# A delta-rule attention with two MLP layers on one core: full-width weight conversion in place, own token staging, masks fused into evacuations, copies that may go to GpSimd

## The chip, the cores and the metric

The kernel runs on one core of one Trainium2 chip. The metric is the device time of one execution in microseconds. TensorE (PE) multiplies, VectorE (DVE), ScalarE (ACT) and GpSimd (POOL) do the elementwise work, SyncE (SP) issues all DMAs.

## What is computed

A delta-rule recurrence over 768 positions for 4 batches of 8 heads with head size 48, and then two MLP layers over all 3072 tokens with a width of 384 and 2048 hidden units. The inputs are float64; the weights come as pairs of 32-bit words and are converted on the core.

```python
for t in range(S):                         # S = 768, state is 48 x 48 per head
    kt, vt, bt = (k_n[:, :, t], v[:, :, t], beta[:, :, t, None])
    y[:, :, t] = np.einsum('bhd,bhde->bhe', q[:, :, t], state)
    v_old = np.einsum('bhde,bhd->bhe', state, kt)
    state = state + bt[:, :, :, None] * np.einsum('bhd,bhe->bhde', kt, vt - v_old)
# x: tokens x 384
h = x @ w_in;  g = np.where(h >= 1, h, np.where(h <= -1, 0, (h + 1) ** 2 / 4));  x = g @ w_out
h = x @ w2_in; g = h * np.clip(h + 3, 0, 6) / 6;                                 x = g @ w2_out
```

`k_n` is k divided by its norm.

## The kernel before

The sequence is cut into 12 chunks of 64 positions. For each chunk `front(c)` loads k twice (once by position into KN, once as tokens into ST), loads q into ST and v into E, takes the norms, transposes the tokens on TensorE, and forms the products of k with k and with q (`products`, two halves of the heads, hb = 0 and 1). `inverse(c)` inverts a triangular matrix for every head: on 32-wide blocks by a row of small multiply and subtract steps (L566, L571; on VectorE for chunk 0, on GpSimd for the rest), and the rest by matmuls. `chain(c)` is the serial part: it computes E from the inverse (L705), the next state, and y, which goes to XB as two parts, a high and a low one. Part of y passes through YS and six small DMAs (L786) into XB.

MLP layer 1 runs in blocks of one chunk (the first two) or two chunks, layer 2 in six blocks of 512 tokens. For each of the 16 slices f of 128 hidden units there are H matmuls (`mlp_h`), a nonlinearity on ScalarE and VectorE (GF, GH, GL), and O matmuls (`mlp_o`). All MLP matmuls are made three times, with weights and activations each split into a high and a low part.

The weights of a slice f are prepared by `wload`: five DMAs (three in layer 2) into a raw buffer (RAWL with four slots, RAWR with one), and then six operations on each half of 384 columns: scale the high words (into TBS), mask the sign bits out of them (L826, into a second buffer), round the low words into 16 bits of that buffer (L828, ScalarE), shift and combine (L831, VectorE), copy the high part into WLA or WLB, subtract to get the low part. Layer 1 is prepared while the first chunks run.

ST has two buffers, so a half's k and q tokens wait until the half before has been transposed. The masked products (p of q with k) are evacuated by ScalarE without a mask (L514) or by VectorE with the mask (L516); for those of ScalarE, a second pass multiplies by the mask in SBUF (L535, VectorE or GpSimd).

The order of everything is made ahead of time by `Plan.emit`. Each operation has a cost, a priority and a choice of engines; the planner puts the operation with the earliest start next, and each engine then runs its queue in that order. Until the first MLP matmul, TensorE's gaps are filled with matmuls on GH that compute nothing. `PR` holds the priorities, and a bias per engine. `cpalt` is a copy that may run on one of several engines, `ttalt` a two-input operation.

```python
AD = PR["ad"]                      # copies: ACT or DVE
DP = PR["dp"]; DW = PR["dw"]       # masks and scalings: DVE or POOL; weight subtraction: DVE
```

Of the kernel before, what the change touches and what calls it, by code (L numbers as in the profile page):

```python
# [37 lines left out]
class Plan:  # L38
# [1104 lines left out]
```

## Time and profile before

| | |
|---|---|
| median of 3 runs | 1086.45 us (1084.42 to 1089.5) |
| profiled execution | 1090.76 us, span 1089.0 us |
| TensorE busy | 1045.1 us (96%) |
| VectorE busy | 662.6 us (61%) |
| ScalarE busy | 595.7 us (55%) |
| GpSimd busy | 277.6 us (25%) |
| TensorE's mean granted clock | 0.983 of 2.4 GHz |

Busy shares over the whole span hide that the stages differ: the attention fronts and the weight conversion lie in the first 600 us and most of all in the first 200, and the end is MLP alone. Times in the rows below are counted from the start of the span. A row of a timeline may hold several equal instructions (x2). A mean in a group is that of one instruction; neighbours on one engine overlap a little, so a sum of means is larger than the busy time. What ended an engine's idle time stands behind the arrow.

### The profile page before, as it was taken

How to read it: one execution, taken by the hardware profiler on the slowest of the kernel's cores; microseconds unless marked ns; L12 is line 12 of the kernel's file. 1: busy time of each engine (PE TensorE's matmuls, PEld its weight loads, DVE VectorE, ACT ScalarE, POOL GpSimd, SP SyncE). 2: the span in 40 equal slices, each digit the busy share in tenths (PEclk: the TensorE clock that was granted, in tenths of full speed). 3: DMA queues.
4: the chain of work that ended last, by engine and by line, in shares of the span. 5: the costliest groups of instructions: out<-in, count | busy, mean ns of one | idle time of the engine just before them, and what ended most of it. 6: DMA issues, size and time to landing. Idle time of an engine off the chain costs nothing.

```text
span 1089.0 us, 25916 instructions
## 1 busy us (share of the span) xinstructions
PE 1045.1 (96%) x10684; PEld 890.1 (82%) x10684; DVE 662.6 (61%) x1258; ACT 595.7 (55%) x1164; POOL 277.6 (25%) x652
## 2 busy tenths in 40 slices
PE   8985899999999999999999999999999999999998
PEld 6764888887777778778778788898999998999897
DVE  4969778777869767786855589533333333333332
ACT  4768686766668576765755689433323232322322
POOL 3022313084755858548460000000000000000000
PEclk9987899999999999999999999999999999999999
DMA  9963243231314303322122284402011020200000
GB/s 179 191 142 66 61 99 66 45 63 36 59 21 97 69 17 59 90 45 46 40 57 83 80 257 139 116 1 88 1 41 47 1 87 2 59 29 1 29 1 29
DMA packets 174757, 71.86 MB, mean 66 GB/s; under 512 B 121264, under 2 KB 170544, under 8 KB 174640
## 3 DMA queue, kind: packets, MB, share of 16 engines
q1 hardware_dynamic: 174640, 70.22, 27.1%
q8 instruction: 84, 1.38, 0.6%
q14 instruction: 33, 0.27, 0.1%
HBM read 53.68 MB, written 14.16 MB: 62 GB/s over the span
## 4 chain that ended last, share of the span: by engine, by line
PE 72%; DVE 11%; ACT 5%; DMA 4%; POOL 3%; issue 3%; SPq 1%; DVEq 0%; POOLq 0%; ACTq 0%
PE bank L389 71%; DMA RAWL<-in_moe_w_in_dram 2%; DVE X L506 2%; POOL TL L571 1%; POOL TMP L566 1%; ACT KQ L514 1%; DVE GF L880 1%; PE bank L471 1%; DVE KQ L535 1%; DMA RAWR<-in_moe_w_in_dram 1%; DVE GL L357 1%; DVE DL L624 1%; ACT G L366 1%; SPq L815 1%; DVE XB L777 1%
## 5 line engine op out<-in xcount | busy, mean ns | idle before, releaser
L389 PE MATMUL bank<-XB,WLA 128*128 128x512 f32 (+1 forms) x1404 | 341.2, 386 | 13.4 <-DMA XB<-YS 7.1
L389 PEld LDWEIGHTS bank<-XB,WLA 128*128 128x128 f32 x1404 | 251.9, 193 | 62.1 <-ACT TBS L828 6.6
L357 DVE TENSOR_TENSOR GL<-GF,GH 128x512 fp32r<-128x512 f32 (+1 forms) x208 | 139.4, 671 | 82.9 <-PE bank L389 57.4
L884 DVE SCALAR_TENSOR_TENSOR GF<-GF,bank 128x512 f32<-128x512 f32 x96 | 66.1, 688 | 193.0 <-ACT GF L883 192.9
L366 ACT ACTIVATE GH<-GF 128x512 fp32r<-128x512 f32 (+1 forms) x202 | 120.9, 599 | 114.3 <-DVE GF L884 69.1
L883 ACT ACTIVATE GF<-bank 128x512 f32<-128x512 f32 x96 | 57.5, 599 | 204.5 <-PE bank L389 203.6
L566 POOL TENSOR_TENSOR TMP<-TL,DL 128x126 f32<-128x126 f32 (+25 forms) x293 | 113.0, 386 | 115.8 <-DVE DL L624 65.7
L571 POOL TENSOR_TENSOR TL<-TL,TMP 128x126 f32<-128x126 f32 (+25 forms) x293 | 126.6, 432 | 23.0
L389 PE MATMUL bank<-GH,WLA 128*128 128x512 f32 (+1 forms) x504 | 121.5, 373 | 2.6 <-DVE GH L368 1.5
L389 PE MATMUL bank<-XB,WLB 128*128 128x512 f32 (+1 forms) x468 | 112.4, 382 | 0.2 <-DVE GF L880 0.2
L389 PE MATMUL bank<-WLA,GH 128*128 128x384 f32 x576 | 112.3, 336 | 0.0
L389 PEld LDWEIGHTS bank<-WLA,GH 128*128 128x128 f32 x576 | 102.8, 188 | 6.4
L389 PEld LDWEIGHTS bank<-GH,WLA 128*128 128x128 f32 x504 | 85.9, 192 | 20.7 <-ACT GH L366 3.5
L389 PEld LDWEIGHTS bank<-XB,WLB 128*128 128x128 f32 x468 | 83.4, 191 | 15.5 <-DVE GF L880 0.4
L880 DVE SCALAR_TENSOR_TENSOR GF<-bank,GF 128x512 f32<-128x512 f32 (+1 forms) x112 | 68.6, 612 | 45.0 <-ACT GF L879 43.8
L878 ACT ACTIVATE GF<-bank 128x512 f32<-128x512 f32 (+1 forms) x112 | 59.8, 534 | 60.6 <-PE bank L389 56.1
L389 PE MATMUL bank<-GL,WLA 128*128 128x512 f32 (+1 forms) x252 | 65.9, 370 | 0.0
L879 ACT ACTIVATE GF<-GF 128x512 f32<-128x512 f32 (+1 forms) x112 | 63.5, 567 | 2.4
L389 PE MATMUL bank<-WLA,GL 128*128 128x384 f32 x288 | 61.5, 334 | 0.0
L389 PEld LDWEIGHTS bank<-WLA,GL 128*128 128x128 f32 x288 | 51.0, 188 | 0.0
L389 PE MATMUL bank<-GH 128*128 128x512 f32 x176 | 50.8, 437 | 0.0
L389 PEld LDWEIGHTS bank<-GL,WLA 128*128 128x128 f32 x252 | 43.9, 191 | 8.2 <-issue 0.3
(135 smaller groups left out, 1357.6 us busy)
## 6 DMA issues: line engine op xcount, KB each, us to landing
XB<-X SPq DMA_DIRECT2D x36, 256.0 KB, 4.7
X<-XB SPq DMA_DIRECT2D x30, 256.0 KB, 2.6
KN<-in_k_dram SPq DMA_DIRECT2D x24, 192.0 KB, 4.0
ST<-in_k_dram SPq DMA_DIRECT2D x48, 96.0 KB, 3.1
ST<-in_q_dram SPq DMA_DIRECT2D x48, 96.0 KB, 3.3
E<-in_v_dram SPq DMA_DIRECT2D x24, 192.0 KB, 3.8
RAWL<-in_moe_w_out_dram SPq DMA_DIRECT2D x12, 384.0 KB, 4.2
KQ<-in_moe_w_in_dram SPq DMA_DIRECT2D x12, 384.0 KB, 5.2
```

What stands on the lines that cost most here:

```text
L357: alts[e] = (d, lambda e=e: ENG[e].tensor_tensor(out=val(out), in0=val(in0), in1=val(in1), op=op))
L366: lambda: nc.scalar.activation(out=val(out), in_=val(in_), func=AF.Copy, scale=scale))
L389: nc.tensor.matmul(o, l, r, start=start, stop=stop)
L471: nc.tensor.transpose(bk.tile[0:112, p * 128:(p + 1) * 128], ST[i][:, p, 0:112], IDN)
L506: P.op("dve", 335, lambda bk=bk, u0=u0, rr=rr, ro=ro: nc.vector.tensor_tensor(out=X[rr, u0:u0 + NP, :], in0=bk.tile[ro].rearrange("p (a x) ...
L566: P.op(te, d, lambda t=t, s=s, r0=r0, a0=a0, a1=a1, m=m: ve.tensor_tensor(out=t[:, a0:a1], in0=TL[:, r0 + a0:r0 + a1, s:s + 1].to_broadcas ...
L571: P.op(te, d, lambda t=t, s=s, r0=r0, a0=a0, a1=a1: ve.tensor_tensor(out=TL[:, r0 + a0:r0 + a1, 0:s], in0=TL[:, r0 + a0:r0 + a1, 0:s], in1 ...
L878: P.op("act", da, lambda: nc.scalar.activation(out=gf, in_=ps, func=AF.Relu, scale=0.5, bias=0.5), r=[hkey(hb)], w=[gk], prio=MP)
L879: P.op("act", da + 48, lambda: nc.scalar.activation(out=gf, in_=gf, func=AF.Square), w=[gk], r=[gk], prio=MP)
L880: P.op("dve", 1.06 * n + 60, lambda: nc.vector.scalar_tensor_tensor(out=gf, in0=ps, scalar=1.0, in1=gf, op0=ALU.max, op1=ALU.min), r=[hkey ...
L883: P.op("act", da, lambda: nc.scalar.activation(out=gf, in_=ps, func=AF.Relu, scale=1.0 / 6.0, bias=0.5), r=[hkey(hb)], w=[gk], prio=MP)
L884: P.op("dve", 1.06 * n + 60, lambda: nc.vector.scalar_tensor_tensor(out=gf, in0=gf, scalar=1.0, in1=ps, op0=ALU.min, op1=ALU.mult), r=[hke ...
```

## The change

Five things change. (1) `wload` converts all 768 columns of a slice at once, so each step is one instruction and not two, and waits for all of the slice's DMAs. The sign bits are masked in place, and the rounded low words are written into the raw buffer too, so the second temporary is gone. The subtraction may also go to GpSimd (`dw`). (2) Chunks 0 and 1 get staging of their own: their second half's k and q tokens go to halves of G[0] and G[1], which are cleared for it, and the zeros that G needs are written later, by `zero_g`. (3) An evacuation of p on ScalarE is charged 500 ns more in the planner's choice (`me`), so more of them go to VectorE with the mask. (4) SBUF copies of X, LT and the diagonal blocks of G may go to GpSimd (`c3`). (5) The planner gets other costs for DMAs, holds back bulk loads while the DMAs are busy (`bulk`, `back`), and has other priorities.

```diff
-PR = dict(kv=-2.451, tok=-1.879, ... bias=27.418, biasa=601.736, hyst=4058, margin=800, dw=('dve',), ...)
+PR = dict(kv=-2.566, tok=-1.896, ... bias=33.201, biasa=369.235, hyst=4974.141, fgap=150, me=500, c3=('act', 'dve', 'pool'), back=1500, margin=251.294, dw=('dve', 'pool'), ...)
...
+                    if o["bulk"]:
+                        t = max(t, dma_free - PR["back"])
...
-                        end = t + o["alts"][e][0] + bias.get(e, 0.0)
+                        ex = o["extra"]
+                        end = t + o["alts"][e][0] + bias.get(e, 0.0) + ex.get(e, 0.0)
...
         for e in engs:
-            if e == "act":
+            if e == "pool":
+                alts[e] = (190 + 1.1 * n, lambda: nc.gpsimd.tensor_copy(val(out), val(in_)))
+            elif e == "act":
...
+    gs = [G[i].rearrange("p u e s -> p (u e s)") for i in range(2)]
+    extra = [gs[0][:, 0:512], gs[0][:, 512:1024], gs[1][:, 1024:1536], gs[1][:, 1536:2048]]
+    ST += [x.rearrange("p (a x) -> p a x", a=NP) for x in extra]
...
-        i = stage[0] % NST
+        if c < 2:
+            i = (0 if hb == 0 else 2 + 2 * c) + stage[0] % 2
+        else:
+            i = stage[0] % NST
...
-                                      q=qd(SH[dl], PO[g][dl], SH[dl]))
+                                      q=qd(SH[dl], PO[g][dl], SH[dl]), extra={"act": PR["me"]})
...
-            cpalt(AD, 256, X[p0:p0 + 32, us, 0:32], X[p0:p0 + 32, us, 32:64], False,
+            cpalt(PR["c3"], 256, X[p0:p0 + 32, us, 0:32], X[p0:p0 + 32, us, 32:64], False,
...
-                cpalt(AD, 512, LT[p0:p0 + 32], X[p0:p0 + 32, :, 32:64], False, ...)
+                cpalt(PR["c3"], 512, LT[p0:p0 + 32], X[p0:p0 + 32, :, 32:64], False, ...)
...
-        for pc in range(2):
...
-            tb, s_ = tmps[n % 2]
-            lw, hw = hl[:, 0, sl[0]:sl[1]], hl[:, 1, sl[0]:sl[1]]
+        tb = tmps[n % 2]
+        lw, hw = hl[:, 0], hl[:, 1]
+        low = raw.bitcast(I16).rearrange("p (n t) -> p t n", t=4)[:, 2]
+        need = [rkey] + [rkey + (i,) for i in range(len(parts))]
+        W = 2 * DM
+        cpalt(AD, W, tb.bitcast(F32), hw.bitcast(F32), False, 2.0 ** -112, r=need, w=[tk], prio=prio)
+        P.op("dve", 67 + 0.53 * W, lambda: V.tensor_scalar(
+            out=hw, in0=hw, scalar1=-2147483648, scalar2=None, op0=ALU.bitwise_and), r=need + [tk], w=[sk], prio=prio, port=("dve",))
+        P.op("act", 110 + 0.835 * W, lambda: nc.scalar.activation(
+            out=low, in_=lw.bitcast(U32), func=AF.Relu, scale=0.875 * 2.0 ** -29, bias=0.49),
+            r=need + [sk], w=[sk], prio=prio)
+        P.op("dve", 64 + 1.05 * W, lambda: V.scalar_tensor_tensor(
+            out=tb, in0=tb, scalar=3, in1=hw, op0=ALU.logical_shift_left, op1=ALU.bitwise_or), ...)
...
+    def zero_g(s_):
+        zk = [("zg", s_)] + [("gw", s_, hb, dl) ...] + tkeys(s_, 0) + tkeys(s_, 1) + [("st", 2 + 2 * s_ + i, b) for i in range(2) for b in range(2)]
+        zero(G[s_][32:64, :, 0, :], zk, 1200)
+        zero(G[s_][32:64, :, 1, 0:32], zk, 600)
+        zero(G[s_][96:128, :, 0, 0:32], zk, 600)
...
+        if c < 2:
+            zero_g(c)
         load_v(c)
```

How the change moves instructions shows at three places. The first is SyncE's queue after the first loads of chunk 0, before (the numbers behind names tell buffers apart: ST_78 and ST_79 are the two buffers of tokens, E_71 and KN_76 are those of even chunks, KN_77 of odd ones):

```order
L411 DMA ST_78<-in_k_dram 64x8x48 x2
L411 DMA ST_79<-in_q_dram 64x8x48 x2
L429 DMA E_71<-in_v_dram 64x16x48 x2
L422 DMA KN_77<-in_k_dram 64x16x48 x2
L815 DMA RAWL<-in_moe_w_in_dram 48x3x256
L815 DMA RAWL<-in_moe_w_in_dram 16x3x256
L815 DMA RAWL<-in_moe_w_in_dram 48x3x256
L815 DMA RAWL<-in_moe_w_in_dram 16x3x256
L411 DMA ST_78<-in_k_dram 64x8x48 x2
L411 DMA ST_79<-in_q_dram 64x8x48 x2
L815 DMA RAWL<-in_moe_w_out_dram 128x768
```

and with the change (here G_74 and G_75 stage tokens):

```order
L442 DMA E_71<-in_v_dram 64x16x48
L424 DMA G_74<-in_k_dram 64x8x48 x2
L424 DMA G_74<-in_q_dram 64x8x48 x2
L442 DMA E_71<-in_v_dram 64x16x48
L435 DMA KN_77<-in_k_dram 64x16x48 x2
L424 DMA ST_78<-in_k_dram 64x8x48 x2
L424 DMA ST_79<-in_q_dram 64x8x48 x2
L424 DMA G_75<-in_k_dram 64x8x48 x2
L424 DMA G_75<-in_q_dram 64x8x48 x2
```

The second half's tokens of chunk 0 stood behind E, KN_77 and the first weights; now they stand behind one half of E.

The second place is VectorE's queue where the small steps of chunk 0's inverse begin (L566 and L571 before, which are L579 and L584 after). Before:

```order
L587 STREAM_TRANSPOSE DL<-X 128x512
L357 TENSOR_TENSOR WLA<-TBS,WLA 128x384
L593 TENSOR_SCALAR DL<-DL,PAR 128x256
L831 SCALAR_TENSOR_TENSOR TBS<-TBS 128x384
L595 SCALAR_TENSOR_TENSOR DL<-DL,PAR 128x256
L368 CAST WLA<-TBS 128x384
L566 TENSOR_TENSOR TMP<-TL,DL 128x15
L357 TENSOR_TENSOR X<-KN_77 128x768
L571 TENSOR_TENSOR TL<-TL,TMP 128x15
L357 TENSOR_TENSOR WLA<-TBS,WLA 128x384
L566 TENSOR_TENSOR TMP<-TL,DL 128x28
L443 TENSOR_REDUCE SM<-X 128x16
```

and with the change:

```order
L606 TENSOR_SCALAR DL<-DL,PAR 128x256
L608 SCALAR_TENSOR_TENSOR DL<-DL,PAR 128x256
L362 TENSOR_TENSOR X<-KN_77 128x768
L579 TENSOR_TENSOR TMP<-TL,DL 128x15
L378 TENSOR_SCALAR TBS<-RAWL 128x768
L584 TENSOR_TENSOR TL<-TL,TMP 128x15
L456 TENSOR_REDUCE SM<-X 128x16
L579 TENSOR_TENSOR TMP<-TL,DL 128x28
L845 TENSOR_SCALAR RAWL<-RAWL 128x768
L584 TENSOR_TENSOR TL<-TL,TMP 128x2x14
L458 TENSOR_SCALAR SM<-SM 128x16
L579 TENSOR_TENSOR TMP<-TL,DL 128x39
```

The first slice's conversion was in progress here, half by half; now its first instruction stands one step into the inverse, and is 768 wide.

The third place is GpSimd's queue ahead of chunk 1's inverse. Before:

```order
L399 MEMSET G_75 32x16x32 x2
L357 ISA
L357 TENSOR_TENSOR E_72<-E_72,NRM_90 64x16x48
L574 MEMSET TL 128x512
L579 MEMSET TL 128x16
L586 MEMSET LT 128x16x16
L566 TENSOR_TENSOR TMP<-TL,DL 128x15
L571 TENSOR_TENSOR TL<-TL,TMP 128x15
```

and with the change:

```order
L409 MEMSET G_74 32x16x32 x2
L409 MEMSET G_75 32x16x64
L409 MEMSET G_75 32x16x32 x2
L548 TENSOR_TENSOR KQ<-KQ,MSK 64x4x64 x4
L587 MEMSET TL 128x512
L592 MEMSET TL 128x16
L370 COPY G_74<-DL 32x16x32
L599 MEMSET LT 128x16x16
L362 TENSOR_TENSOR WLA<-TBS,WLA 128x768
L579 TENSOR_TENSOR TMP<-TL,DL 128x15
L584 TENSOR_TENSOR TL<-TL,TMP 128x15
```

GpSimd now masks four blocks, copies a block of G and subtracts one slice's weights before the steps of the inverse.

## Rows read from the trace of the kernel before

**Rows 1.** Busy time by stretch, columns: start:end, length, engines, PEclk, DMA, GB/s

```profile
0.00:26.00 26.00, 21.07 (x143) 16.58 (x144) 10.78 (x24) 12.63 (x23) 9.42 (x20) 1.00 0.94 179
26.00:76.00 50.00, 44.67 (x633) 34.49 (x632) 41.80 (x113) 36.66 (x76) 5.21 (x9) 0.93 0.87 185
76.00:128.00 52.00, 35.75 (x804) 31.59 (x800) 41.86 (x95) 39.96 (x89) 12.16 (x38) 0.77 0.28 59
128.00:221.00 93.00, 87.72 (x1884) 81.25 (x1880) 74.27 (x167) 66.75 (x157) 23.72 (x71) 0.96 0.33 66
221.00:272.00 51.00, 48.91 (x619) 40.06 (x619) 37.77 (x72) 32.32 (x68) 33.21 (x76) 1.00 0.27 52
272.00:1089.00 817.00, 807.03 (x6627) 686.14 (x6623) 456.15 (x788) 407.33 (x753) 193.83 (x441) 1.00 0.21 56
```

**Rows 2.** Timeline of VectorE: start us, us, instruction, idle before and its releaser

```profile
26.10 0.87 DVE L506 TENSOR_TENSOR X<-bank,D 128x256 f32<-128x256 f32 x2 [0.24 <-ACT KQ L514]
...
76.20 2.32 DVE L705 TENSOR_TENSOR E<-bank,D 64x384 f32<-64x384 f32 x4 [1.50 <-PE bank L389]
...
272.50 2.31 DVE L705 TENSOR_TENSOR E<-bank,D 64x384 f32<-64x384 f32 x4 [0.90 <-PE bank L389]
```

**Rows 3.** What VectorE waited for, 76 to 272 us: total, times, longest

```profile
DVE GF L880 <- ACT GF L879: 10.6, 11, 3.5
...
DVE KQ L516 <- ACT KQ L514: 0.5, 1, 0.5
```

**Rows 4.** Timeline of SyncE's DMA issues

```profile
7.45 1.36 SPq L429 DMA_DIRECT2D E<-in_v_dram  x2
...
13.55 1.28 SPq L411 DMA_DIRECT2D ST<-in_k_dram  x2
```

**Rows 5.** VectorE groups, 0 to 272 us: count, busy us, mean ns, idle

```profile
L831 DVE SCALAR_TENSOR_TENSOR TBS<-TBS 128x384 int32<-128x384 int32 x32 | 17.3, 549 | 7.4 <-ACT TBS L828 7.3
L535 DVE TENSOR_TENSOR KQ<-KQ,MSK 64x512 f32<-64x512 f32 x20 | 13.8, 688 | 1.6 <-ACT KQ L514 1.3
L826 DVE TENSOR_SCALAR TBS<-RAWL 128x384 int32<-128x384 int32 x24 | 9.9, 414 | 0.9 <-DMA RAWL<-in_moe_w_in_dram 0.7
L357 DVE TENSOR_TENSOR X<-KN 128x768 f32<-128x768 f32 x5 | 4.8, 951 | 2.3 <-DMA KN<-in_k_dram 2.2
L516 DVE TENSOR_TENSOR KQ<-bank,MSK 64x256 f32<-64x256 f32 x1 | 0.4, 426 | 0.5 <-ACT KQ L514 0.5
```

**Rows 6.** ScalarE groups, 0 to 272 us

```profile
L514 ACT ACTIVATE KQ<-bank 64x256 f32<-64x256 f32 x47 | 17.8, 379 | 8.3 <-DVE X L506 5.3 <-PE bank L389 2.1
L828 ACT ACTIVATE TBS<-RAWL 128x384 int16<-128x384 uint32 x24 | 14.4, 629 | 0.0
L879 ACT ACTIVATE GF<-GF 128x256 f32<-128x256 f32 x32 | 13.2, 412 | 0.6
L366 ACT ACTIVATE TBS<-RAWL 128x384 f32<-128x384 f32 x21 | 11.2, 548 | 2.4 <-DVE WLA L357 2.1
L366 ACT ACTIVATE WLA<-TBS 128x384 fp32r<-128x384 f32 x20 | 10.1, 518 | 3.2 <-DVE TBS L831 2.8
L879 ACT ACTIVATE GF<-GF 128x512 f32<-128x512 f32 x6 | 3.8, 631 | 0.2
```

**Rows 7.** A GpSimd group, whole span

```profile
L357 POOL TENSOR_TENSOR E<-E,NRM 64x768 f32<-64x768 f32 x3 | 5.6, 1872 | 33.0 <-DVE X L506 32.9
```

**Rows 8.** Timeline at 43 us; then GL of VectorE, 359 to 410 and 640 to 1080

```profile
43.10 2.67 POOL L357 TENSOR_TENSOR E<-E,NRM 64x768 f32<-64x768 f32 x1 [32.92 <-DVE X L506]
...
44.35 1.63 DVE L826 TENSOR_SCALAR TBS<-RAWL 128x384 int32<-128x384 int32 x1
...
L357 DVE TENSOR_TENSOR GL<-GF,GH 128x512 fp32r<-128x512 f32 x9 | 6.6, 735 | 2.6 <-ACT GH L366 2.6
...
L357 DVE TENSOR_TENSOR GL<-GF,GH 128x512 fp32r<-128x512 f32 x105 | 72.6, 692 | 63.5 <-PE bank L389 55.3 <-ACT GH L366 8.1
```

**Rows 9.** A TensorE group, whole span: layer-1 matmuls of 256 columns

```profile
L389 PE MATMUL bank<-XB,WLA 128*128 128x256 f32 x216 | 38.2, 322 | 9.9 <-DMA XB<-YS 7.1 <-issue 1.5 <-DVE GF L880 1.2
```

More of the change, by code (lines that the diff above doesn't have):

```diff
@@ L47, in __init__, with op @@
         self.tag = ""
-    def op(self, eng, dur, fn, r=(), w=(), prio=0.0, pre=(), alloc=(), uses=(), nbytes=0, own=(), crit=False, alts=None, dyn=None, load=0.5, port=(), tiled=False, q=(0, 0, 0), urgent=False):
+    def op(self, eng, dur, fn, r=(), w=(), prio=0.0, pre=(), alloc=(), uses=(), nbytes=0, own=(), crit=False, alts=None, dyn=None, load=0.5, port=(), tiled=False, q=(0, 0, 0), urgent=False, bulk=False, extra=None):
         i = len(self.ops)
@@ L69, in op @@
         self.ops.append(dict(eng=eng, dur=dur, fn=fn, deps=deps, prio=prio, alloc=alloc, uses=us, nbytes=nbytes, own=own, crit=crit, tag=self.tag,
-                             alts=alts or {eng: (dur, fn)}, dyn=dyn, load=load, port=port, tiled=tiled, q=q, urgent=urgent))
+                             alts=alts or {eng: (dur, fn)}, dyn=dyn, load=load, port=port, tiled=tiled, q=q, urgent=urgent, bulk=bulk, extra=extra or {}))
         return i
@@ L167, in emit @@
                     if len(o["alts"]) > 1:
-                        end = t + o["alts"][e][0] + bias.get(e, 0.0)
-                        if any(max(free[x], ready[i], port_free if x in o["port"] else 0.0) + d + bias.get(x, 0.0) < end
+                        ex = o["extra"]
+                        end = t + o["alts"][e][0] + bias.get(e, 0.0) + ex.get(e, 0.0)
+                        if any(max(free[x], ready[i], port_free if x in o["port"] else 0.0) + d + bias.get(x, 0.0) + ex.get(x, 0.0) < end
                                for x, (d, _) in o["alts"].items() if x != e):
@@ L175, in emit @@
                         cand = k
-                if cand is not None and HOLD and e == "dve":
-                    lim = cand[0] + HOLD
+                if cand is not None and PR["dh"] and e == "dve":
+                    lim = cand[0] + PR["dh"]
                     end = cand[0] + ops[cand[3]]["alts"][e][0]
@@ L837, in wload @@
-        P.op("none", 0, lambda: None, r=[tk], w=[rkey])
+            P.dma(lambda o=o, a=a: nc.sync.dma_start(out=o, in_=a), rows * KT, rows * 1024 * KT * (nf if i < len(parts) - 1 else KT),
+                  w=[rkey + (i,)], pre=[rkey], prio=prio, bulk=perm,
+                  cost={48: 620.0, 16: 310.0}.get(rows))
+        f = fs[0]
+        n = wcount[0]
+        wcount[0] += 1
+        tk, sk = ("tb", n % 2), rkey + ("s",)
+        tb = tmps[n % 2]
+        hl = raw.rearrange("p (n t) -> p t n", t=2)
@@ new lines, in wload @@
+        P.op("dve", 64 + 1.05 * W, lambda: V.scalar_tensor_tensor(
+            out=tb, in0=tb, scalar=3, in1=hw, op0=ALU.logical_shift_left, op1=ALU.bitwise_or),
+            r=[tk, sk], w=[tk], prio=prio, port=("dve",))
+        cpalt(AD, W, lambda: wl(f, 0, 0, W), tb.bitcast(F32), False, r=[tk, ("wlb", f >= NFA)], w=[("w", f, pc, 0) for pc in range(2)], prio=prio)
+        ttalt(DW, W, lambda: wl(f, 1, 0, W), tb.bitcast(F32), lambda: wl(f, 0, 0, W).bitcast(F32), ALU.subtract,
+              r=[tk] + [("w", f, pc, 0) for pc in range(2)], w=[("w", f, pc, 1) for pc in range(2)], prio=prio)
@@ L1023, in open_xb1 @@
         XB[1] = open_pool("xb1", "right").tile([128, KT, 2, 512], F32R, name="XB1")
-    tmps1 = [(TBS[:, 2 * i, :], TBS[:, 2 * i + 1, :]) for i in range(2)]
+    tmps1 = [TBS[:, i, :] for i in range(2)]
     for f in range(NF):
@@ L1036, in fused_kernel @@
     raws2 = [kq[:, 1536 * i:1536 * i + 1536] for i in range(3)] + [g0[:, 0:1536]]
-    tmps2 = [(g1[:, 2 * DM * i:2 * DM * i + DM], g1[:, 2 * DM * i + DM:2 * DM * i + 2 * DM]) for i in range(2)]
+    tmps2 = [g1[:, 2 * DM * i:2 * DM * i + 2 * DM] for i in range(2)]
     def xkeys_of(cs):
```

86 lines of the change are left out of this document (36 added, 50 removed).

## Prediction

> **What bounds the kernel now.** I began with the busy time by stretch, cut where the first chunks finish [rows 1]. From 272 us on TensorE is busy 807.03 of 817 us at the full clock of 2.4 GHz: whatever VectorE, ScalarE or GpSimd save there, at most those 10 us can come back, and most of them lie in the last drain. Before 272 it is otherwise. The stretch 76 to 128 has 35.75 busy us of 52 at a granted clock of 0.77, so part of it at 1.2 GHz; from 128 to 272 TensorE is busy 136.6 of 144. Up to 76 us its busy time is largely the filler matmuls on GH, which compute nothing. So only the first 272 us can pay, and mostly the first 128.
>
> Next I asked what TensorE waits for there. The timeline of VectorE has three landmarks [rows 2]: at 26.10 it first evacuates the second half's products of chunk 0, at 76.20 it writes E of chunk 0 (L705), at 272.50 E of chunk 4. Between 26 and 76 VectorE is busy 41.80 of 50 us and ScalarE 36.66; between 76 and 128 they are busy 41.86 and 39.96 of 52 [rows 1]. Two engines at about 80% that hand each piece of work to one another leave little room: this stage goes at their pace. The waits say the same: of VectorE's waits between 76 and 272 us the largest is for ScalarE's square, 10.6 us [rows 3]. Weight conversion is the bulk that could go. Before 26 us it is the loads: DMA share 0.94, and the tokens of chunk 0's second half are issued only at 13.55 us, after E, the next KN and four weight transfers [rows 4].
>
> **The change part by part.** The sum is made against the profiled execution (span 1089.0, time 1090.76) and taken off the median, 1086.45, which lies 4.3 below it. The counts are those of the order, up to the first L705 of chunk 4 on VectorE and the first YS of chunk 4 on ScalarE, times the mean of the form.
>
> *Own staging.* The second half of chunk 0 no longer waits until the first half's transposes free ST, and its four loads move ahead of KN and of all weights, just behind one half of E, issued from 7.45 on [rows 4]. Issues take 0.65 us each, so they leave at about 8.1 to 10.8 us and not 13.55 to 16.2: 5.4 earlier. The products need ScalarE's three evacuations of the first half first, which I put at 16 us, so the second half's evacuation falls at 20 to 22 rather than 26.10 [rows 2]. Ends: 0 (another load is last) and -5.7; I take -5, because the queue in front of them shrinks by just that. Past that point VectorE has as much work up to E of chunk 0 as before (48.3 against 48.0 us by forms), so the 5 us stay. What is moved back is the weights: their first issue slides from 11.05 to some 18 us. VectorE's first conversion stands in order behind its first inverse step, which it reaches at about 26 us, when the first weights should be down (2.75 MB of tokens at the 179 to 185 GB/s of [rows 1] take 15 us from 3 us on, 0.79 MB of weights 4 more: 22, and the landing).
>
> *Weights at 768.* Before, one f costs VectorE two each of L826, L831 and the subtraction, a two-input pass of 384 like L831: 2 x (0.414 + 0.549 + 0.549) = 3.02 us; ScalarE 2 x (0.629 + 0.548 + 0.518) = 3.39 [rows 5, 6]. At 768 a two-input pass takes 0.951 by the row of X<-KN [rows 5]; the masking pass of one input 0.57 (0.414, or 0.36 without its one long case, plus 384 elements at 0.55 ns). That is 2.47 us. On ScalarE 256 more elements cost 0.219 [rows 6], so 384 cost 0.33: 0.96 + 0.88 + 0.85 = 2.69. Over the 16 f's of layer 1, with four subtractions that the order now gives to GpSimd, and fewer copies on VectorE: 51.3 to 39.0, -12.3 us on VectorE; 49.0 to 38.1, -10.9 on ScalarE. The masking pass now writes every other word in place, which no row shows. If it runs at the pace of a two-input pass (0.951) it costs 0.38 x 16 = 6.1 us more; below nothing it can't go, as it has as many elements. I take 0.57, since its strided reads already run at that pace. Likewise ScalarE's L847 lies between 0.96 and twice 0.629, at most 4.8 us more in all.
>
> *Fused masks.* By chunk 4, 19 evacuations go from L514 on ScalarE (0.379) to L516 on VectorE (0.426), which masks as it reads. VectorE: +8.0, less 13 wide masks of 0.688 (-9.0), plus six narrow ones (+2.5): +1.5. ScalarE: -7.2 [rows 5, 6].
>
> *Copies and the rest.* Up to chunk 4 eight copies go to GpSimd, three scalings of E too (768 of two inputs, 0.951 on VectorE, 1.872 on GpSimd [rows 5, 7]), and new priorities hand some evacuations from ScalarE to VectorE: VectorE +2.1, ScalarE -8.2. Together VectorE has 227.7 - 8.7 us to do, ScalarE 200.3 - 26.3. Of the 8.7, 3.1 lie ahead of the second product, where VectorE waited anyway; -5.6 count. (Lengths of neighbours overlap: by stretches VectorE is busy 206 of the 228.)
>
> *Less ScalarE.* Of VectorE's waits between 76 and 272 30 us are for ScalarE, in 13 rows from 10.6 down to 0.5 [rows 3]. Its work in this stage falls by 19 of 150, 13%. Ends: 0, and -15 if half of the waits go; I take 13% of 30, -4.
>
> *GpSimd.* It gets 17 us more of work that reads SBUF by chunk 4 (four subtractions and three scalings at 1.9, eight copies, masks). No row shows it copying 512 elements: between ScalarE's 0.63 and 1.25, its product's share [rows 7]; I take 0.8. Its own time is free: 83.7 busy of 272 us [rows 1]. What it costs others shows in two places. At 43.10 its product took 2.67 and not 1.87, and the masking pass beside it on VectorE 1.63 and not 0.35; yet GL in a stretch where GpSimd works on an inverse takes 0.735, against 0.692 where it is done [rows 8]. By the first, 17 us cost 17 x 1.28/2.67 = 8; by the second under 1. I take +2, nearer to the many than to the one.
>
> The Trainium skill has a rule against this part (SBUF — State Buffer, section Who interferes with whom): VectorE and GpSimd share one pair of ports, held for a whole instruction, and whoever comes second is blocked, not slowed. The 1.63 agrees; by that rule alone any of the 17 us could fall on VectorE in full.
>
> *After 272 us.* The matmuls are the same 4032, and chunk 4's E stands behind as many of them as before; TensorE has no gap to give. 0, from -4 to +3.
>
> Sum: -5 - 5.6 - 4 + 2 + 0 = -12.6. 1090.76 - 12.6 = 1078.2; off the median 1073.9, so **1074 us**. TensorE can follow: from 76 to 272 it has 172.4 us of work in 196 [rows 1]. The new order puts 144 instead of 81 layer-1 matmuls of 256 columns ahead of chunk 1's E, 63 x 0.177 = 11 us [rows 9] into a stretch with 16 idle; that is done later otherwise, so I count nothing for it.
>
> **Rivals.**
> *Hidden anyway.* TensorE is the bound already from 128 us (137 of 144), and the cut of VectorE and ScalarE buys nothing behind the first stretch: only the earlier tokens stay, -5 + 2 = -3, **1083**. For it: the share of TensorE; against it: 0.96 of the clock and the 16 idle us before 128.
> *More than shares.* ScalarE was what VectorE waited for, and half the 30 us go, with no charge for GpSimd: -5 - 5.6 - 15 = -26, **1061**. For it: rows 3 are nearly all ScalarE; against: single passes of 0.96 us now stand in front of short urgent ones.
> *Slower: the shared port.* GpSimd and VectorE block each other as at 43.10, each time. Then all 17 us fall on VectorE, the masking pass loses its fast pace (+6), and the inverse of chunks 1 to 3 on GpSimd, 90 short steps, waits for passes of 0.95 where they were 0.55, which at one step in four and 0.4 us is 3 a chunk, 9: -14.6 + 17 + 6 + 9 = +17, **1104**. It decides from the point where the loss passes 14.6 + 5.4 = 20 us. Against it: the planner keeps these passes apart as it sees them, and GL's 0.043.
> That nothing moves is no rival: the order shows the 768-wide passes, the early loads and 20 copies on GpSimd.
>
> **How the numbers follow.** Forecast, 1068 to 1081: 0.50. More than shares, below 1068: 0.17. Hidden, 1081 to 1092: 0.21. Slower, above 1092: 0.12. Half a per cent, 5.4 us, is about what a measurement of this kernel can tell from no change: below 1081.0 is faster, 0.67; up to 1091.9 the same, 0.21; above it slower, 0.12. The range takes 1057 at the low end (-29: the best ends of all terms, short of 1 us) and 1092 at the high end (the new passes at their dear ends, +11, and GpSimd at 8): outside lie 0.04 and 0.12.
>
> **What would show it.** Right: L519 evacuates the second product before 23 us, E of chunk 0 (L718) comes near 71, E of chunk 4 near 260, and the 12 us are there by then and neither grow nor shrink. The masking pass L845 near 0.57, L847 near 0.96, VectorE's busy time up to chunk 4 down by 5 to 9, ScalarE's by some 25. Wrong: L845 near 0.95, VectorE passes over a microsecond beside GpSimd, VectorE waiting for weights inside the first inverse, or chunk 4's E near 272 although both engines have less to do.

## The result, and the profile after

The changed kernel takes **1096.81 us** (median of 4 runs, 1096.28 to 1098.2), beside 1087.45 for the kernel before: ratio 1.008, interval 1.0055 to 1.0105. It is 0.8% slower; the forecast was 1074, with a range that ended at 1092. In a second measurement (the run e9 below) the ratio was 1.0049 (1.0029 to 1.0068). The profiled execution has a span of 1094.5 us; before it was 1089.0.

The busy time by stretch answers to [rows 1]; the row from 272 on is cut in three, so that 624 to 700 stands alone, and 640 to 690 is asked once more by itself.

```profile
0.00:26.00 26.00, 19.25 (x140) 14.64 (x141) 13.27 (x30) 13.62 (x25) 10.92 (x22) 1.00 0.78 147
26.00:76.00 50.00, 41.84 (x630) 33.18 (x628) 40.13 (x89) 36.92 (x45) 11.38 (x12) 0.86 0.91 206
76.00:128.00 52.00, 36.03 (x701) 32.45 (x700) 40.44 (x75) 36.48 (x60) 17.90 (x39) 0.71 0.31 66
128.00:221.00 93.00, 87.77 (x1980) 81.23 (x1978) 78.16 (x170) 66.93 (x149) 35.13 (x91) 1.00 0.32 60
221.00:272.00 51.00, 48.54 (x696) 39.32 (x695) 38.80 (x72) 30.12 (x62) 33.55 (x79) 1.00 0.27 52
272.00:624.00 352.00, 347.67 (x4266) 276.22 (x4260) 259.89 (x453) 216.02 (x403) 200.19 (x448) 1.00 0.28 63
624.00:700.00 76.00, 69.49 (x290) 52.43 (x289) 56.91 (x82) 67.08 (x81) 1.84 (x1) 1.00 0.43 138
700.00:1094.50 394.50, 389.89 (x1960) 352.29 (x1958) 136.40 (x202) 120.20 (x200) 0.00 (x0) 1.00 0.11 34
...
640.00:690.00 50.00, 43.49 (x172) 30.72 (x172) 39.51 (x57) 49.76 (x58) 0.00 (x0) 1.00 0.38 130
```

The same two stretches of the kernel before, which the prediction did not ask for:

```profile
624.00:700.00 76.00, 76.00 (x337) 62.55 (x337) 63.01 (x133) 60.95 (x124) 0.00 (x0) 1.00 0.56 175
...
640.00:690.00 50.00, 50.00 (x220) 40.70 (x219) 47.48 (x105) 46.08 (x96) 0.00 (x0) 1.00 0.47 153
```

Between 640 and 690 us, the first block of layer 2, the weights of layer 2 are converted. TensorE fell there from 50.00 to 43.49 busy us, and ScalarE rose from 46.08 to 49.76 of 50. In the 76 us around it TensorE made 290 matmuls instead of 337: 47 fewer, at 76.00/337 = 0.226 us each some 10 us of work that is done later.

The landmarks on VectorE, answering to [rows 2]:

```profile
19.95 0.87 DVE L519 TENSOR_TENSOR X<-bank,D 128x256 f32<-128x256 f32 x2 [0.65 <-PE bank L396]
...
76.01 1.14 DVE L718 TENSOR_TENSOR E<-bank,D 64x384 f32<-64x384 f32 x2
...
268.03 2.32 DVE L718 TENSOR_TENSOR E<-bank,D 64x384 f32<-64x384 f32 x4 [0.40 <-PE bank L396]
```

The second product came 6.1 us earlier than before (26.10), E of chunk 0 did not (76.20 before), and E of chunk 4 came 4.5 us earlier (272.50 before). So, in these two profiles: -4.5 by chunk 4, and +10.0 behind it (826.5 us instead of 816.5), as much as layer 2's first block lost; the spans differ by +5.5. The medians lie 9.4 us apart. The profile of the kernel before is 3.3 us above its median, so little of the 4.5 may be real.

ScalarE's groups of the low-word step in layer 2 (624 to 692 us) and in layer 1 (0 to 272 us), columns as in [rows 6]; the last two are those of the kernel before in layer 2 (624 to 692 us), on halves:

```profile
L847 ACT ACTIVATE KQ<-KQ 128x768 int16<-128x768 uint32 x10 | 19.0, 1960 | 0.0
L847 ACT ACTIVATE G<-G 128x768 int16<-128x768 uint32 x4 | 7.9, 1976 | 0.0
...
L847 ACT ACTIVATE RAWL<-RAWL 128x768 int16<-128x768 uint32 x12 | 22.8, 1939 | 6.7 <-DVE RAWL L845 6.7
L847 ACT ACTIVATE RAWR<-RAWR 128x768 int16<-128x768 uint32 x4 | 7.7, 1936 | 0.0
...
L828 ACT ACTIVATE G<-KQ 128x384 int16<-128x384 uint32 x19 | 11.2, 632 | 0.0
L828 ACT ACTIVATE G<-G 128x384 int16<-128x384 uint32 x8 | 4.8, 632 | 0.0
```

I had put it at 0.96, at most 1.26. It takes 1.94 to 1.98 on average, 32 times.

### The profile page after: what moved, and what is told of

Its sections match the earlier page's. It is cut to its first block, busy times and chain, and to the rows that moved or that the text cites. A ratio compares the mean times of both kernels' runs of the same rounds, so it can differ in the third digit from the quotient of the medians.

```text
span 1094.5 us, 25616 instructions
## 1 busy us (share of the span) xinstructions
PE 1040.5 (95%) x10645; PEld 881.8 (81%) x10645; DVE 664.0 (61%) x1171; ACT 587.4 (54%) x1020; POOL 310.9 (28%) x689
## 4 chain that ended last, share of the span: by engine, by line
PE 71%; ACT 10%; DVE 8%; POOL 3%; issue 3%; DMA 3%; SPq 2%; DVEq 0%; ACTq 0%; POOLq 0%
PE bank L396 70%; ACT KQ L847 2%; SPq L831 1%; POOL TMP L579 1%; POOL TL L584 1%; PE bank L484 1%; ACT G L373 1%; ACT GF L897 1%; ACT RAWL L847 1%; DMA RAWL<-in_moe_w_out_dram 1%; ACT GF L898 1%; DVE XB L790 1%; DMA RAWL<-in_moe_w_in_dram 1%; ACT XB L373 1%; DVE GL L362 1%
## 5 line engine op out<-in xcount | busy, mean ns | idle before, releaser
L373 ACT ACTIVATE GH<-GF 128x512 fp32r<-128x512 f32 (+1 forms) x198 | 118.4, 599 | 130.3 <-DVE GF L903 71.6
L579 POOL TENSOR_TENSOR TMP<-TL,DL 128x126 f32<-128x126 f32 (+25 forms) x293 | 122.4, 418 | 80.0 <-DVE DL L637 36.8
L584 POOL TENSOR_TENSOR TL<-TL,TMP 128x126 f32<-128x126 f32 (+25 forms) x293 | 119.1, 406 | 22.9
L373 ACT ACTIVATE KQ<-bank 48x512 f32<-48x512 f32 (+1 forms) x66 | 39.0, 591 | 9.2 <-PE bank L484 8.0
```

The source lines that it names most:

```text
L373: lambda: nc.scalar.activation(out=val(out), in_=val(in_), func=AF.Copy, scale=scale))
L579: P.op(te, d, lambda t=t, s=s, r0=r0, a0=a0, a1=a1, m=m: ve.tensor_tensor(out=t[:, a0:a1], in0=TL[:, r0 + a0:r0 + a1, s:s + 1].to_broadcas ...
L584: P.op(te, d, lambda t=t, s=s, r0=r0, a0=a0, a1=a1: ve.tensor_tensor(out=TL[:, r0 + a0:r0 + a1, 0:s], in0=TL[:, r0 + a0:r0 + a1, 0:s], in1 ...
```

## The experiments

E of chunks 0 and 4 is the first write on VectorE, TensorE's busy time that between 624 and 700 us; ratios are to the kernel before on the same chip. "Order moved" means that the planner planned anew, as it also did in e6, e11, e12 and e15; the other runs keep the changed kernel's queue on every engine, but for what they take out or put in. "Low words left out" means that ScalarE writes them where VectorE's combination does not look for them.

| run | us | ratio (interval) | E c0 | E c4 | TensorE 624:700 |
|---|---|---|---|---|---|
| e9 changed kernel again | 1094.95 | 1.0049 (1.0029, 1.0068) | 74.9 | 266.1 | 69.48 |
| e2 layer 2 apart | 1084.91 | 0.9955 (0.9933, 0.9976) | 73.9 | 264.9 | 75.91 |
| e3 whole words, low words left out | 1080.25 | 0.9906 (0.9881, 0.993) | 77.5 | 261.5 | 75.91 |
| e4 apart + words, order moved | 1095.57 | 1.0056 (1.0034, 1.0078) | 78.0 | 267.3 | 75.72 |
| e5 RAWR reused, order moved | 1095.99 | 1.0066 (1.0041, 1.0091) | 74.5 | 273.8 | 75.71 |
| e6 price told to the planner | 1091.59 | 1.0018 (0.9997, 1.0039) | 73.5 | 276.2 | 74.97 |
| e7 e3 without own staging, order moved | 1095.42 | 1.0046 (1.0025, 1.0068) | 78.3 | 267.7 | 75.75 |
| e8 e3 without GpSimd copies, order moved | 1086.3 | 0.9964 (0.9942, 0.9985) | 75.6 | 267.3 | 75.96 |
| e10 whole version, order kept | 1084.27 | 0.9964 (0.9939, 0.9989) | 77.2 | 268.9 | 75.94 |
| e11 e3, margin nudged | 1079.93 | 0.9911 (0.9877, 0.9945) | 74.4 | 258.6 | 75.95 |
| e12 e3, biasa nudged | 1085.91 | 0.9978 (0.9955, 1.0001) | 74.3 | 268.6 | 75.95 |
| e13 e3, GpSimd cut short | 1077.91 | 0.99 (0.9857, 0.9942) | 77.2 | 260.2 | 75.93 |
| e14 e3, shared buffers, order kept | 1088.72 | 0.9996 (0.9973, 1.0019) | 83.5 | 267.9 | 75.94 |
| e15 e10, margin nudged | 1090.09 | 1.0008 (0.9983, 1.0033) | 75.6 | 267.4 | 75.93 |

### The price of the form (e1)

> A kernel that runs only the forms of the low-word step on ScalarE, one after the other and with nothing beside them, and the masking forms on VectorE; it computes none of the reference. Source always the low words (768 words at 8-byte steps). Theory (the 2-byte write at 8-byte steps is what costs): into another buffer at 8-byte steps 1.94 us, in place 1.94 too, at 4-byte steps about 0.96, whole words at 8-byte steps about 0.95 in place and elsewhere; 384 elements at 8-byte steps about 1.05. Rival (reading and writing the same words costs): into another buffer at 8-byte steps about 0.96, and in place 1.94 with 2-byte and with whole-word writes alike.

ScalarE's groups of that kernel (WORD is written at 4-byte steps, HALF without gaps, RAW at 8-byte steps; three of each six RAW rows write over their own source, three another buffer):

```profile
L325 ACT ACTIVATE RAW<-RAW 128x768 int16<-128x768 uint32 x6 | 11.4, 1895 | 0.0
L325 ACT ACTIVATE RAW<-RAW 128x384 int16<-128x384 uint32 x6 | 6.3, 1050 | 0.1
L325 ACT ACTIVATE RAW<-RAW 128x768 int32<-128x768 uint32 x6 | 5.4, 892 | 0.1
L325 ACT ACTIVATE WORD<-RAW 128x768 int16<-128x768 uint32 x3 | 3.3, 1107 | 0.0
...
L325 ACT ACTIVATE HALF<-RAW 128x768 int16<-128x768 uint32 x3 | 2.7, 906 | 3.1 <-DMA RAW<-in_moe_w_in_dram 3.1
L325 ACT ACTIVATE WORD<-RAW 128x384 int16<-128x384 uint32 x3 | 1.9, 623 | 0.0
```

It is the 2-byte write with gaps, in place or not (the six lie between 1.87 and 1.95): 1.895 at 8-byte steps, 1.107 at 4, 0.906 without gaps; whole words at 8-byte steps cost 0.892. From 384 to 768 elements the step grows by 2.2 ns an element at 8-byte steps and 1.26 at 4. The width of 768 is worth 0.14 us a step while the result stays at 4-byte steps (2 x 0.623 against 1.107), half of what I had taken (2 x 0.629 against 0.96), and the new place of the result costs 0.79.

The Trainium skill (SBUF — State Buffer, section Door 1: The DMA port swizzle) explains cliffs of strided access, measured on GpSimd, by lines of 16 bytes that want two hits each. Half words and whole words at 8-byte steps touch the same lines, two to a line; 1.895 against 0.892 is not told by that rule.

### Layer 2 alone (e2)

```diff
-        low = raw.bitcast(I16).rearrange("p (n t) -> p t n", t=4)[:, 2]
+        low = sx.bitcast(I16).rearrange("p (n t) -> p t n", t=2)[:, 0]   # layer 2: sx = KN[n % 2]
-            out=hw, in0=hw, ...            # mask
+            out=sx, in0=hw, ...
```

> The changed kernel, but in layer 2 the sign bits and low words go to two buffers of their own (the two KN tiles, dead by then) at 4-byte steps; order of all engines unchanged. Theory (ScalarE is the bound of layer 2's first block, because its low-word step takes 1.96 and not 0.96): the step falls to about 1.0 us x 16, ScalarE is busy some 9 us less between 630 and 690, TensorE's lost 9 to 10 us come back: 1096.8 - 9.5 = 1087 (1084 to 1090). Rival (the wide passes come too late or too coarsely there, whoever runs them): ScalarE idles instead, TensorE still waits, 1093 to 1097.

The two stretches, and its group of the low-word step:

```profile
624.00:700.00 76.00, 75.91 (x340) 62.06 (x339) 60.46 (x91) 59.20 (x86) 1.85 (x1) 1.00 0.49 154
640.00:690.00 50.00, 49.99 (x220) 40.17 (x219) 40.07 (x61) 40.78 (x61) 1.85 (x1) 1.00 0.41 136
...
L852 ACT ACTIVATE KN<-KQ 128x768 int16<-128x768 uint32 x10 | 10.5, 1080 | 0.0
```

With 1.08 instead of 1.96 ScalarE is busy 40.78 of 50 and TensorE 49.99: the block's loss is gone, and the kernel, 10 us faster than in e9, beats the one before. VectorE's masks went to the new buffers too; but e3 (next), which changes ScalarE's write alone, gives the same 75.91 of 76. That ScalarE's dear form was the loss in this block is shown by the two together.

### Both layers (e3)

```diff
-            out=low, in_=lw.bitcast(U32), func=AF.Relu, ...
+            out=lw, in_=lw.bitcast(U32), func=AF.Relu, ...
```

> The changed kernel, but ScalarE writes the low words as whole 32-bit words over the low words themselves, in both layers, so that VectorE's combination leaves them out (the low parts of the weights are wrong); order and all else unchanged. Theory: the step takes about 0.95 in both layers; 9.5 us come back in layer 2 and, since ScalarE has 16 us less up to chunk 4, another 4 to 8 before 272 us: 1079 to 1084. Rival (the front lost its gain to GpSimd's blocking of VectorE and to passes of 0.95 us between the short steps of the inverse): nothing more than layer 2's share, 1086 to 1090, and E of chunk 4 stays near 268.

```profile
L847 ACT ACTIVATE RAWL<-RAWL 128x768 int32<-128x768 uint32 x12 | 10.8, 920 | 0.0
...
261.47 2.32 DVE L718 TENSOR_TENSOR E<-bank,D 64x384 f32<-64x384 f32 x4 [0.40 <-PE bank L396]
...
76.00:128.00 52.00, 41.02 (x839) 37.37 (x838) 45.31 (x88) 36.93 (x71) 22.78 (x39) 0.77 0.34 70
624.00:700.00 76.00, 75.91 (x345) 63.25 (x344) 58.80 (x88) 55.42 (x83) 1.85 (x1) 1.00 0.46 146
```

With 0.92 in layer 1 too, another 4.7 us (1084.91 to 1080.25) come back, and E of chunk 4 falls at 261.5, where I had put it (near 260). In the profiles 3.4 of them lie ahead of it (264.9 in e2); that alone says little, since three profiles under one order have it at 268.0, 266.1 and 264.9. But between 76 and 128 us TensorE is busy 41.02 of 52 here, and 36.73 in e2 (36.03 in the result's profile). The front and the block together are 14.7 us against e9 (by the ratios 1.43%, 15.6 us).

### Could the planner have avoided it? (e6)

```diff
-        P.op("act", 110 + 0.835 * W, ...   # low words
+        P.op("act", 110 + 2.38 * W, ...
```

> The changed kernel, but the planner is told the measured price of the low-word step (1.94 us instead of 0.75); the form stays. Theory (in layer 2's first block ScalarE has more work than the block lasts, whatever the order): the 9 us of that block stay lost, 1092 to 1100. Rival (the loss is that the planner put work too late, since it counted 1.2 us too few per step): it recovers to 1083 to 1089.

```profile
624.00:700.00 76.00, 74.97 (x322) 59.44 (x322) 65.83 (x102) 63.21 (x75) 0.00 (x0) 1.00 0.49 153
```

My theory was too strong. With the true price the planner hands copies to VectorE (65.83 busy, 56.91 in the changed kernel), and the block loses 1 us of TensorE's busy time, not 6.5, and 15 matmuls, not 47. So the block's loss is the dear form under an order that did not know its price. But the front moved too, E of chunk 4 to 276.2, and the kernel stays no faster than the one before.

### Own staging (e7, e14) and orders (e11, e12)

```diff
-        if c < 2:                                  # e7: planned without staging
+        if False:
             i = (0 if hb == 0 else 2 + 2 * c) + stage[0] % 2
...
-    ST += [x.rearrange("p (a x) -> p a x", a=NP) for x in extra]
+    ST += [ST[0], ST[1], ST[0], ST[1]]             # e14: order kept, buffers shared
```

e14 also leaves out the clearing of G's staging halves.

> As the run with whole words (low words left out of the weights, 1080.25), but chunks 0 and 1 without staging of their own: all tokens go through the two ST buffers again. Theory of the prediction (own staging is worth 5 us that stay): 1083 to 1088. Rival (the 6 us that the second product comes earlier are lost again inside chunk 0's inverse, where VectorE's wide passes stand between the short steps): 1078 to 1082.

> As the run with whole words (1080.25), same order on every engine, but the staging of chunks 0 and 1 in G is taken away: the same loads, at their place in the queue, go to the two ST buffers, and wait there until the transposes before them have read. Theory of the prediction (own staging is worth 5 us that stay): second product of chunk 0 back near 25 us, 1083 to 1087. Rival (the early second product is used up inside chunk 0's inverse): E of chunk 0 unchanged at 77, 1079 to 1082.

Of e14, SyncE's loads of chunk 0's second half and of chunk 1's first tokens (k), TensorE's first transposes, and on VectorE the norm ahead of the first product, and the second product:

```profile
8.51 1.29 SPq L424 DMA_DIRECT2D ST<-in_k_dram  x2
...
12.75 1.07 PE L484 MATMUL bank<-IDN,ST 128*112 128x128 f32 x4 [5.28 <-DMA ST<-in_k_dram]
...
13.86 5.58 SPq L424 DMA_DIRECT2D ST<-in_k_dram  x2
...
16.02 0.25 DVE L460 RECIPROCAL SM<-SM 128x16 f32<-128x16 f32 x1 [5.86 <-ACT SM L459]
...
24.78 0.87 DVE L519 TENSOR_TENSOR X<-bank,D 128x256 f32<-128x256 f32 x2 [0.65 <-PE bank L396]
```

e14 did not do what I expected of it. The loads of the second half did not wait for the first half's transposes: they left at 8.51 into the same two buffers, and the transposes waited for them, until 12.75 (9.39 in e3). So even the first product falls late, at 19.84 (15.78 in e3), behind a wait of 5.86 us for ScalarE's root, and the first half works on the wrong tokens. Only chunk 1's loads wait as meant: SyncE stands for 5.58 us with all weights behind it. e14's 6.0 us at E of chunk 0 (83.5 against 77.5) and 8.5 in all are therefore no price of the buffers; they show that under this order a second product that is 3.6 us late, with weights 4.6 us late (24.01 and 19.41), is not made up.

e7 is the run that bears on the staging. Planned without it, E of chunk 0 comes at 78.3 and E of chunk 1 at 127.80 (129.1 in e3): nothing lost by then that single profiles could tell. e7's 15 us (13 in the profiles) arise after chunk 1: 6 by E of chunk 4, where TensorE is busy 84.82 of 93 between 128 and 221 at a clock of 0.96 (88.57 at 1.00 in e3), and 7 behind it, with TensorE busy 25.74 of 30 at a clock of 0.94 between 450 and 480 (30.00 at 1.00). How much an order alone does, two nudges show that take no work away (a few instructions change their engine):

```diff
-margin=251.294        # e11          -biasa=369.235        # e12
+margin=260                           +biasa=375
```

> As the run with whole words (1080.25), with the same instructions' costs and choices, but one of the planner's numbers nudged (margin 251.294 to 260), which by itself changes no work and only leads the planner to another order. Theory (the runs without staging, without GpSimd copies and with RAWR reused lost mostly by another order, not by what was taken away): this one loses too, 1084 to 1096. Rival (order is worth little, those three lost by what was taken away): 1079 to 1082.

> As the run before it, with another nudge (biasa 369.235 to 375). Theory (another order by itself costs): 1084 to 1096. Rival: 1079 to 1082.

One nudge cost nothing, the other 5.7 us, again at 128 to 221 (86.00 busy, clock 0.94). So 6 us is within what another order does; e7's 15 are beyond the two nudges seen, but they arise where orders differ, and what they are due to stays open.

### GpSimd (e8, e13)

```diff
-c3=('act', 'dve', 'pool'), ... dw=('dve', 'pool')          # e8
+c3=('act', 'dve'), ... dw=('dve',)
...
-ENG[e].tensor_tensor(out=o, in0=o, in1=m, ...)              # e13, for GpSimd; scalings of E likewise
+ENG[e].tensor_tensor(out=o[:, 0:1], in0=o[:, 0:1], in1=m[:, 0:1], ...)
```

> As the run with whole words (1080.25), but copies and weight subtractions are not offered to GpSimd; masks and scalings of E still may go there. VectorE and ScalarE get 20 copies and 5 subtractions back, some 15 us over the whole kernel, half of it before 272 us. Theory of the prediction (GpSimd costs the others 2 us and takes more off them): 1081 to 1086. Rival (blocking beside GpSimd costs VectorE more than the copies are worth): 1073 to 1078, and fewer VectorE instructions above their usual length.

> As the run with whole words (1080.25), same order on every engine, but GpSimd's masks (14) and its scalings of E (7) work on the first column only, so that their results are incomplete: GpSimd has some 22 us less that reads SBUF, two thirds of it before 272 us. Theory of the prediction (GpSimd's new work costs the others about 2 us): 1077 to 1080. Rival (VectorE and GpSimd block each other for the whole of it): 1064 to 1072. Chunk 0's inverse on VectorE, 23.2 us there, should be shorter by the 2 us that its small steps take longer beside GpSimd's masks.

e8's 6 us are no more than a nudge. e13 cut less than meant (GpSimd 118.36 to 112.90 busy us before 272, 315.20 to 299.30 in all, since the 14 masks, on one column, still took 0.658 us on average, 0.977 before), and its 2.3 us lie inside the intervals. With 5.5 us taken away it cannot exclude that GpSimd's new work costs the others all of its 17. What speaks against that is e3: it has all of this work, and its E of chunk 4 still comes 11.0 us earlier than before.

### Whole versions (e4, e5, e10, e15), and the run to run spread (e9)

e4 and e10 let ScalarE write whole words in layer 1 and VectorE join them in one two-input pass, with layer 2 as in e2; in e4 the planner orders anew, in e10 the order of the changed kernel is kept. e5 keeps the words at 4-byte steps, in RAWR. e15 is e10 in e11's order.

```diff
+            V.scalar_tensor_tensor(out=hw, in0=hw, scalar=-2147483648, in1=lw, op0=ALU.bitwise_and, op1=ALU.bitwise_or)
             V.scalar_tensor_tensor(out=tb, in0=tb, scalar=3, in1=hw, op0=ALU.logical_shift_left, op1=ALU.bitwise_or)
```

> A whole version: layer 2 as in the run with buffers apart; in layer 1 ScalarE writes whole words in place, and VectorE masks the high words and joins the low ones in one two-input pass of 0.95 (it was 0.56). VectorE has 6 us more than in the changed kernel up to chunk 4, ScalarE 16 less; the planner's order moves with it. Theory: 1080 to 1086, below the kernel before. Rival (VectorE is the bound of the front): the 6 us come on top of layer 2's repair, 1088 to 1094.

> A whole version without the dear form: sign bits and low words go to 4-byte steps in a buffer of their own, in layer 2 the two KN tiles, in layer 1 the halves of RAWR for slices 0 to 11 (RAWR is idle until slice 12); slices 12 to 15 stay in place. RAWR's first load then waits for slice 11, and the planner's order moves with it. Theory (the low-word step was the whole loss): 28 steps at 1.1 instead of 1.95 take 24 us off ScalarE, 1079 to 1086. Rival (the order moved by the planner costs as much as the form gives): 1088 to 1096.

> A whole version that keeps the changed kernel's order: layer 2 with the KN tiles as buffers apart; in layer 1 ScalarE writes whole words in place, the masking pass is dropped from its place, and at the place of the combination VectorE makes two two-input passes (mask and join the low words; shift and combine). ScalarE has 16 us less than the changed kernel up to chunk 4, VectorE 6 us more. Theory (the dear form was the loss, and the order is what keeps the gain): 1080 to 1085, ratio about 0.993. Rival (VectorE bounds the front, its 6 us come on top of the run with layer 2 apart): 1086 to 1092.

> The whole version that keeps the changed kernel's order (1084.27), with the nudged margin of 260: in the run with whole words this order had E of chunk 4 at 258.6 instead of 261.5. Theory (the order carries over): 1080 to 1085. Rival (with VectorE's longer passes the order's lead is lost): 1085 to 1090.

> The changed kernel itself, beside the next three on the same chip, to see how much its first 100 us differ from run to run under one order: in its first profile E of chunk 1 came at 134.7, in the run with layer 2's buffers apart, whose order up to there is the same, at 131.4. Expected 1.006 to 1.010 of the kernel before and E of chunk 1 between 130 and 136, with TensorE's 9 us lost again between 624 and 700.

e2 and e10 are whole and beat both kernels: ratios 0.9955 and 0.9964. So e10's repair of layer 1 adds nothing that shows to that of layer 2. e4, e5 and e15 have the same repair of layer 2 (75.7 to 75.9 of 76) and lose it elsewhere. e4 and e5 lose it between 128 and 221 us, where TensorE is busy 81.85 of 93 at a clock of 0.89 and 83.13 at 0.96 (87.89 at 1.00 in e2). Why e5's front is so late (E of chunk 1 at 138.6) was not followed up: its RAWR loads wait as well, and its order is new. e15 has E of chunk 4 no later than e10 and takes 3 us more behind it; its theory fell, and the cause is open. In e9 E of chunk 1 came at 132.6, after 134.7 and 131.4 under one order: differences of up to 3 us at one landmark of single profiles say nothing.

Of the expectations, those of e1 (but for 4-byte steps: 1.107, not 0.96), e2 and e3 held, and those of e10 (but for its ratio), e12 and e13. e5, e11 and e15 went with the rival, e6 and e8 missed both ranges narrowly, e4, e7 and e14 fell outside both, and e9's ratio lies below the one expected.

## Why the prediction was wrong, point by point

**The step that failed** is the price of the low-word step in "weights at 768": "L847 lies between 0.96 and twice 0.629, at most 4.8 us more in all". It measures 1.94: 0.98 x 16 = 15.7 us more in layer 1, and 14 such steps in layer 2's block. My upper bound was no bound. The row of L828 [rows 6] writes at 4-byte steps into a buffer of its own; the diff moves the result into the raw buffer, at 8-byte steps, and I priced only the width, and that by rows of 4-byte results (0.96, where e1 has 1.107 at 4-byte steps). I asked that very question of VectorE's masking pass (in place, every other word) and not of ScalarE's. By e3 and e9 the term is worth 1.43%, of the 1.6 to 2.0% by which the forecast (0.9885) missed the two measurements (1.0049 and 1.008).

**After 272 us: 0, from -4 to +3.** Wrong by the same term. The row 272 to 1089 [rows 1] with 807 of 817 let me treat the rest as TensorE's. Inside it lies a block in which ScalarE had 46.08 and VectorE 47.48 of 50; 14 steps at 1.96 where 27 took 0.632 (624 to 692 us) are 27 us instead of 17, and ScalarE had 4 to give. A stage with no idle TensorE can still be one step from another engine's bound, and a cut was needed there as much as at 76 and 128.

**Less ScalarE, -4.** Of the 26 us it was to lose up to chunk 4, 16 came back through L847: between 0 and 272 us it is busy 184.1 us (188.3 before). With these gone (e3, 175.1 busy) the run gives 4.7 us more than e2.

**Weights on VectorE.** Right in price: L845 has a median of 0.562 (12 rows on RAWL, one of 1.183), L850 0.962, so it is not the in-place write as such that is dear. VectorE's sum did not fall by 5 to 9: between 0 and 272 it is busy 210.8 us (206.5 before), with chunk 4 4.5 us further on.

**Own staging, -5.** The second product came as forecast (19.95; I said 20 to 22), and "the 5 us stay" failed: E of chunk 0 comes at 76.0, 74.9 and 73.9 in the three profiles under this order (76.2 before; I said 71). Chunk 0's inverse begins at 26.69 instead of 32.43 and ends at 53.58 instead of 52.73. By the rows of VectorE's timeline between its first and last step, overlaps taken off, weights take 10.8 us in it (7.3 before), its own 30 steps 5.8 (4.0), and 3.9 are idle (0.9). Its ends, with the change and before, then some of its rows with the change, VectorE's and GpSimd's:

```profile
26.69 0.17 DVE L579 TENSOR_TENSOR TMP<-TL,DL 128x15 f32<-128x15 f32 x1
...
53.39 0.19 DVE L584 TENSOR_TENSOR TL<-TL,TMP 128x15 f32<-128x15 f32 x1
...
32.43 0.17 DVE L566 TENSOR_TENSOR TMP<-TL,DL 128x15 f32<-128x15 f32 x1
...
52.56 0.17 DVE L571 TENSOR_TENSOR TL<-TL,TMP 128x15 f32<-128x15 f32 x1
```

```profile
27.89 0.56 DVE L378 TENSOR_SCALAR TBS<-RAWL 128x768 f32<-128x768 f32 x1 [1.04 <-DMA RAWL<-in_moe_w_out_dram]
...
33.73 0.55 DVE L584 TENSOR_TENSOR TL<-TL,TMP 128x55 f32<-128x55 f32 x1
...
34.29 0.94 DVE L850 SCALAR_TENSOR_TENSOR TBS<-TBS,RAWL 128x768 int32<-128x768 int32 x1
35.16 0.74 DVE L579 TENSOR_TENSOR TMP<-TL,DL 128x60 f32<-128x60 f32 x1
...
48.01 0.96 DVE L850 SCALAR_TENSOR_TENSOR TBS<-TBS,RAWL 128x768 int32<-128x768 int32 x1 [0.86 <-ACT RAWL L847]
48.88 0.19 DVE L579 TENSOR_TENSOR TMP<-TL,DL 128x39 f32<-128x39 f32 x1
49.77 0.97 DVE L850 SCALAR_TENSOR_TENSOR TBS<-TBS,RAWL 128x768 int32<-128x768 int32 x1 [0.70 <-ACT RAWL L847]
...
33.48 0.73 POOL L548 TENSOR_TENSOR KQ<-KQ,MSK 64x256 f32<-64x256 f32 x1 [1.86 <-issue]
34.27 1.56 POOL L548 TENSOR_TENSOR KQ<-KQ,MSK 64x256 f32<-64x256 f32 x1
38.91 1.73 POOL L548 TENSOR_TENSOR KQ<-KQ,MSK 64x256 f32<-64x256 f32 x1 [3.09 <-ACT KQ L527]
40.71 0.73 POOL L548 TENSOR_TENSOR KQ<-KQ,MSK 64x256 f32<-64x256 f32 x1
```

The weights that VectorE did before in its wait for the second product now stand inside the inverse, the steps of about 0.2 us grow to 0.55 and 0.74 beside GpSimd's masks, and weight passes that wait for ScalarE, and the first one for its weights (1.04 us at 27.89), hold up the short steps queued behind them. In e3, where L847 takes 0.92, the idle time in the inverse falls to 0.9 us and the whole of it from 26.9 to 23.2. Equal work up to a landmark does not keep a gain: the idle time ahead of it was filling itself with that work.

**GpSimd, +2.** Near, although its work grew by 25 us before 272 us (83.7 to 108.9 busy) and not by 17. In the rows above, VectorE's step at 33.73 ends when the mask of 33.48 does; the mask of 34.27 takes 1.56 and not 0.73, as it ends only after L850, which ran beside it; and VectorE's step at 35.16 ends when that mask does. The masks of 38.91 and 40.71 do the same once more. This agrees with the rule of the Trainium skill that the prediction cites (SBUF — State Buffer, section Who interferes with whom): whoever comes second stands until the other is done. So both pay: VectorE's 30 steps took 1.8 us more, GpSimd's four masks 1.8 too, and in e13, with the masks cut short, the steps took 4.1 us (5.7 in e3). Few instructions meet in this way: over all of VectorE up to 272 us, what instructions beside GpSimd took beyond the median of their form adds up to some 6 us, against 3 before (an estimate from the rows of the two traces).

**The rivals.** The measured time lies between "hidden anyway" (1083) and "slower: the shared port" (1104), and neither is its cause: the port's 17 us are not there, and in layer 2's first block TensorE waited for ScalarE instead of being the bound. The sum itself holds better than its result: with the low-word step near the price that I took (0.92, e3), the ratio is 0.9906, and the forecast's 1074/1086.45 is 0.9885, inside e3's interval. That is in part luck. In e3 E of chunk 0 comes at 77.5, 6 us later than I said, and from there to E of chunk 4 it takes 183.9 us, where I had put 189: the gain did not come where the terms put it.

## What to carry to other kernels

A form's price belongs to the element size and the steps of its result, not only to its count: when a diff moves a result to another place, look for a row that writes there, and if there is none, the bound above is not the old price. Cut the profile into stretches wherever the set of running work changes, also where the bounding engine is dense, and ask in each how much the second and third engine have left; an instruction made dearer is paid in every stage that runs it. Under a planner, check that its costs are the measured ones, and expect a few microseconds either way from any new order before crediting the edit.

## What was not expected of the hardware

ScalarE writes 2-byte results with gaps more slowly, at 8-byte steps at half the pace: 768 of them take 0.906 us without gaps, 1.107 at 4-byte steps and 1.895 at 8-byte steps, while 4-byte results at 8-byte steps take 0.892. VectorE's in-place masking of every other word costs 0.562, as much as into a buffer without gaps (0.560 in e1's kernel).
